# Attention scores by head on 64 rows of the matmul array each, 128 queries at a time, with one maximum for both heads

## The chip, the cores and the metric

The kernel runs on one core of one Trainium2 chip. The metric is the device time of one execution in microseconds. Before the change the median of three runs is 1036.53 us (1034.72 to 1038.2).

## The reference, cut to what matters

Batch 4, 8 heads, 576 positions, head width 64. Each head's attention output is mixed with a memory readout, and the result goes through two dense feed-forward layers (512 to 2048 to 512, over 2304 tokens).

```python
scores = scale * np.matmul(q, k.transpose(0, 1, 3, 2))        # scale = 1/8
scores = np.where(causal, -1000000000.0, scores)              # causal: key after query
a = np.exp(scores - scores.max(-1, keepdims=True))
a /= a.sum(-1, keepdims=True) + 1e-09
local = np.matmul(a, v)
mem_out = (phi(q) @ M_prev) / (phi(q) . z_prev + 1e-6)        # phi(x) = elu(x) + 1
x = g * mem_out + (1 - g) * local                             # g = sigmoid(beta), by head
h = x @ w_in;  x = (h * sigmoid(h)) @ w_out                   # first layer
h = x @ w2_in; y = (h * tanh(softplus(h))) @ w2_out           # second layer
```

## The kernel before

**Stages.** The heads are worked in 16 pairs: the two heads of a pair lie one above the other on the 128 partitions (64 of head width each). A *visit* is a pair with some of its query tiles, a *step* is one tile of 128 queries of a visit (qt = 0 to 4; the last has 64 queries). Batch 0 is visited twice, first for qt 0 and 1 of its four pairs (steps 0 to 7), then for qt 2 to 4 (steps 8 to 19); batches 1 to 3 follow pair by pair with all five (steps 20 to 79). A step goes through `stage_a` (scores, maximum, exponentials, a split of the result into two float16 parts, and a DMA that transposes them), `stage_b` (times v, the memory product, normalization) and, every second step, `stage_c` (transpose by TensorE, then a DMA to `xd` in DRAM).

The first layer reads `xd` in nine *chunks* of 256 tokens, each with 8 steps of `gemm1`, `hidden` and `gemm2`. Chunk 1 needs qt 2 and 3 of all four pairs of batch 0, chunk 2 needs qt 4 of these and qt 0 and 1 of all four pairs of batch 1. The weights of both layers are loaded, scaled and split by ScalarE and VectorE ahead of use; those of the first layer are prepared beside the first twenty steps. The second layer starts when the first is done.

**Scores before (L495 to L551).** A step works on two tiles of 64 queries. For each, the stationary operand has 128 columns in which the queries of the two heads alternate (`"p q e -> p (q e)"`), with zeros where a column's head is not that of the partition, so that one product over all 128 rows gives both heads' scores, 64 queries by 2 heads on the 128 output partitions. A tile i has 64(i+1) keys. For qt 0 and 1 the product is in float32 (TensorE runs it as two passes); for qt 2 to 4 both operands are split into two fp32r parts and three products are added. A last product of `ident16` with a 64-column `mask` adds the causal mask. Then, by tile, VectorE takes the maximum (L538, with a read of its accumulator behind it), ScalarE the exponentials (L543), ScalarE or VectorE the first float16 part (L545) and VectorE the rest (L546).

The operands with their zeros are prepared by `prep_q` (L448): a copy for each head, and for qt 2 to 4 the rest by GpSimd or VectorE (`rest`, L356).

**PSUM.** Scores of steps 0 to 7 take turns over four banks (2 to 5, `s_all`), those of later steps over two (4 and 5, `s_few`, L789). The two tiles of qt 0 or 1 share one bank; each tile of qt 2 and 3 takes one; qt 4 (576 keys) takes two.

**Order.** All instructions are handed to `Plan`, which puts them in order by a simulation of the engines with given costs: the operation with the lowest priority value that is ready goes next. On TensorE attention goes ahead of `gemm1` and `gemm2` (priority 1e6 and more); on ScalarE and VectorE the work of the first layer (`MOE_B`, -1e6) and of the weights goes ahead of attention from step 8 on. Each engine then runs its list in order. `mm` (L360) gives the planner the cost of products.

Of the kernel before, what the change touches and what calls it, by code (L numbers as in the profile page):

```python
# [173 lines left out]
def attn_moe_moe2_kernel(ctx: ExitStack, tc: tile.TileContext, kq, vm, beta, w1, w2, out):  # L174
# [22 lines left out]
    def buf(name, shape, dt, n=1):  # L197
        ts = [sb.tile([128, *shape], dt, name=f"{name}_{i}") for i in range(n)]
        return ts

    def ring(tiles):
        state = [0]

        def take():
            state[0] += 1
            return tiles[(state[0] - 1) % len(tiles)]

        return take
# [5 lines left out]

    ident, = buf("ident", [128], F32)
    ident16, = buf("ident16", [128], BF16)
    mask, = buf("mask", [D], BF16)
    gb, = buf("gb", [H], F32)
    gv, = buf("gv", [H // 2, 4], F32)
    eps, = buf("eps", [4], F32)  # L220
# [46 lines left out]
    pt_tile, = carve([PT_BLOCKS, 128], F16)  # L267
    kqr, rmr, rvr = ring(carve([2, S], F32, 2)), ring(carve([130], F32, 3)), ring(carve([VM - 130], F32, 2))
    khr, klr = ring(carve([S], F32R, 2)), ring(carve([S], F32R, 2))
    q_parts = [(0, 4), (4, 5)]  # L270
    qz = [[carve([4, D, 2], F32) for _ in range(2)], [carve([5, D, 2], F32R, 2)]]
    qr = [ring(t) for t in qz]
    v1s, v2s = carve([NQ, 2, D + 2], F16, 2), carve([NQ, 2, D], F16, 2)
    v1r, v2r = ring(v1s), ring(v2s)
    scales = carve([4], F32, 3)
    scr, topr, scaler, gvr = ring(scales), ring(carve([2], BF16, 3)), ring(carve([1], F32, 3)), ring(carve([4], F32, 3))
    er_ = ring(carve([S], F32, 2))
    jr = ring(carve([576], BF16))
    pr, phr = ring(carve([640], F32, 4)), ring(carve([16, 128], F16, 3))
    mr = ring(carve([1], F32, 4))  # L280
    t4r = ring(carve([2, 4, D], F32))
    denr, xr = ring(carve([2, 4], F32, 2)), ring(carve([2, 2, D], F32))
    xor_ = ring(carve([256], F32, 2))
# [14 lines left out]
    def cols(a):  # L298
        n = 1
        for x in a.shape[1:]:  # L300
            n *= x
        return n
# [53 lines left out]
    def rest(prio, out, in_, hi, es=("POOL", "DVE")):  # L356

        tt(prio, out, in_, hi, ALU.subtract, es)

    def mm(prio, ms, whole=False):  # L360

        ns, edge, before = 0, None, 0
        for o, _, r, _, _ in ms:
            n = cols(o)
            load, one, times = (107, 2 * n / 2.4 + 2.5, 2) if r.dtype == F32 else (107 if r.dtype == F32R else 14, n / 2.4 + 2.5, 1)
            for _ in range(times):
                ns += one + (0 if edge is None else max(0, load - before))
                edge = (edge or (load, 0))[0], one
                before = one

        def go():
            for o, l, r, a, z in ms:
                nc.tensor.matmul(out=o, lhsT=l, rhs=r, start=a, stop=z)  # L373

        writes = [m[0] for m in ms]
        if whole:
            writes = [(t, 0, 128, b0 // 2048 * 2048, -(-b1 // 2048) * 2048) for t, _, _, b0, b1 in map(plan.region, writes)]
        plan.add(prio, [("PE", ns, go)], writes, [x for m in ms for x in m[1:3]], edge=edge)
# [13 lines left out]
    def setup():  # L392
        p = -1e9
        other(p, "SP", 100, lambda: nc.scalar.dma_start(out=gb, in_=beta), [gb])
        for x, t in enumerate([t for j in qz for i in j for t in i]):
            for r, e in ((slice(0, 64), 1), (slice(64, 128), 0)):
                o = t[r, :, :, e].bitcast(F32)
                plan.add(p + x, [
                    ("DVE", 0.52 * cols(o) + 68, lambda o=o: nc.vector.memset(o, 0.0)),
                    ("POOL", 1.0 * cols(o) + 60, lambda o=o: nc.gpsimd.memset(o, 0.0))], [t[r]], [])  # L400

        def consts():
            make_identity(nc, ident16)
            nc.gpsimd.memset(mask, 0.0)

            nc.gpsimd.affine_select(
                out=mask, in_=mask, compare_op=ALU.is_ge, fill=-8e9, base=0,
                pattern=[[-2, D]], channel_multiplier=1)
            make_identity(nc, ident)
            nc.gpsimd.memset(eps[:, 0:2], 1e-9 * PSCALE)  # L410
            nc.gpsimd.memset(eps[:, 2:4], 1e-6)
            nc.gpsimd.memset(ones, 1.0)
            nc.gpsimd.memset(onesf, 1.0)
            for t in scales:
                nc.gpsimd.memset(t[:, 2:4], 1.0)
            for t in v1s:
                nc.gpsimd.memset(t[:, :, :, D:D + 1], 1.0)

        other(p, "POOL", 2000, consts, [ident16, mask, ident, eps, ones, onesf, *scales, *v1s])
        act(p, gb, gb, AF.Tanh, 0.5)  # L420
        g3 = gb.rearrange("p (a h) -> p a h", h=2)
        ts(p, gv[:, :, 0:2], g3, -0.5, ALU.mult, 0.5, ALU.add)
        ts(p, gv[:, :, 2:4], g3, 0.5, ALU.mult, 0.5, ALU.add)
# [22 lines left out]
        dma(prio, rm[v], vm[p, :, 0:130], reads=[])  # L446

    def prep_q(v, j, prio):  # L448
        i0, n = q_parts[j]
        parts = qq[v, j] = qr[j]()  # L450
        for e in range(2):
            r = slice(64 * e, 64 * e + 64)
            src = rq[v][r, 64 * i0:64 * (i0 + n)].rearrange("p (i q) -> p i q", q=64)
            hi = parts[0][r, :, :, e]
            copy(prio, hi, src)
            if j:
                rest(prio, parts[1][r, :, :, e], src, hi, QL)

    def prep_k(v, prio):
        n = min(S, 128 * VISITS[v][2])  # L460
# [34 lines left out]
    def stage_a(n, sbk, prio):  # L495

        v, qt = STEPS[n]
        kh, kl = kk.get(v, (None, None))
        tiles = [i for i in (2 * qt, 2 * qt + 1) if i < S // 64]
        nk = qt + 1  # L500
        nb = 2 * len(tiles) * nk
        ph = phr()[:, 0:nb, :]
        pv = ph.rearrange("p (s k t) c -> p s k t c", s=2, k=nk)

        ns = [64 * (i + 1) for i in tiles]
        one_bank = sum(ns) <= 512
        scs, masks, ms = [], [], []
        for t, (i, N) in enumerate(zip(tiles, ns)):
            if N > 512 and turn[0] % 2:
                turn[0] += 1  # L510
            off = 0
            if t and one_bank:
                off = ns[0]
            else:
                bk = sbk[turn[0] % len(sbk)]
                turn[0] += 1 if N <= 512 else 2
            sc = bk[0][:, bk[1] + off:bk[1] + off + N]
            scs.append(sc)
            j = 0 if i < 4 else 1
            qs = [x[:, i - q_parts[j][0]].rearrange("p q e -> p (q e)") for x in qq[v, j]]  # L520
            new = not (t and one_bank)
            m = []
            for a, z in [(0, min(N, 512))] + ([(512, N)] if N > 512 else []):
                if j == 0:
                    m.append((sc[:, a:z], qs[0], rk[v][:, a:z], new, False))
                else:
                    m += [(sc[:, a:z], qs[0], kh[:, a:z], new, False), (sc[:, a:z], qs[0], kl[:, a:z], False, False),
                          (sc[:, a:z], qs[1], kh[:, a:z], False, z < N)]
            ms.append(m)
            masks.append((sc[:, N - 64:N], ident16, mask, False, not one_bank or t == len(tiles) - 1))  # L530
        if one_bank:
            mm(prio, sum(ms, []) + masks)
        else:
            for m, x in zip(ms, masks):
                mm(prio, m + [x])
        for t, (N, sc) in enumerate(zip(ns, scs)):
            m1, junk, P = mr(), jr()[:, 0:N], pr()
            other(prio, "DVE", 1.04 * N + 225, lambda m1=m1, sc=sc, junk=junk: nc.vector.tensor_scalar(  # L538
                out=junk, in0=sc, scalar1=-0.125, scalar2=None, op0=ALU.mult, op1=ALU.min, accum_out=m1), [m1, junk], [sc])
            if N < 128 * nk:  # L540
                pad = P[:, N:128 * nk]
                other(prio, "POOL", 90, lambda pad=pad: nc.gpsimd.memset(pad, 0.0), [pad])
            act(prio, P[:, 0:N], sc, AF.Exp, 0.125, m1)  # L543
            Pv = P[:, 0:128 * nk].rearrange("p (k c) -> p k c", c=128)
            copy(prio + D_S, pv[:, 0, :, t, :], Pv, PSCALE)  # L545
            stt(prio + D_S, pv[:, 1, :, t, :], Pv, PSCALE, pv[:, 0, :, t, :], ALU.mult, ALU.subtract)  # L546

        live = pt_live[1 - LAG:]
        p0 = next(x for x in [pt_live[-1][1], 0] + [z for _, z in live] if x + nb <= PT_BLOCKS and all(
            z <= x or x + nb <= a for a, z in live))  # L550
        pt_live.append((p0, p0 + nb))  # L551
        pt = pts[n] = pt_tile[:, p0:p0 + nb, :]
        plan.add(prio, [("SP", max(1180, 400 + 113 * nb), lambda: nc.sync.dma_start_transpose(
            out=pt, in_=ph.rearrange("p n c -> p (n c)")))], [pt], [ph], tail=112 * nb)
# [5 lines left out]
    def stage_b(n, prio):  # L560
# [3 lines left out]
        nk = qt + 1  # L564
        v1, v2, gvv = vv[v]
        vb = bank[6 + qt % 2]
        pw = pts.pop(n).rearrange("p (s k t) (q e) -> p s k e (t q)", s=2, k=nk, e=2)
        ms = []
        for e in range(2):
            o = vb[0:R, 65 * e:65 * e + 65]  # L570
# [215 lines left out]
    load_kq(0, -1e8)  # L786
    setup()

    s_all, s_few = [[(banks, 512 * i) for i in r] for r in (range(2, 6), range(4, 6))]  # L789
    prep(0, -1e6)  # L790
    load_vm(0, -1e6)

# [111 lines left out]
```

## Time and profile before

| | |
|---|---|
| median of three runs | 1036.53 us |
| profiled execution | 1037.78 us |
| its span, first to last instruction | 1036.0 us |
| granted TensorE clock, mean | 0.965 |
| TensorE busy | 952.9 us (92%) |
| VectorE, ScalarE, GpSimd busy | 645.3, 659.1, 295.9 us |

The span is what the trace covers; the run's time is 1.8 us more. Busy times are unions of an engine's instructions. A product's recorded duration contains its way through the array, so what a product costs a busy TensorE is read from the start of one to the start of the next.

### The profile page before, as it was taken

The page shows a single profiled execution, that of the slowest core. Times are in us where ns is not written, and L with a number is a line of the kernel's source. Part 1 is how long each engine was busy: PE and PEld are TensorE (multiplying, and loading weights), DVE is VectorE, ACT ScalarE, POOL GpSimd, SP SyncE. Part 2 cuts the span into 40 slices and gives each one's busy share as a digit, 9 for nine tenths or more (in the row PEclk, how much of TensorE's full clock was granted, in tenths as well). Part 3 has the DMA queues.
Part 4 walks back from the last instruction along what each step waited for, and adds up shares of the span by engine and source line. Part 5 has one row for each costly group of instructions (what it writes and reads, how often), then busy time and mean ns, then how long its engine had stood idle before and what let it go on. Part 6 is the DMA issues. An engine that isn't in the chain of part 4 may idle for free.

```text
span 1036.0 us, 20987 instructions
## 1 busy us (share of the span) xinstructions
PE 952.9 (92%) x8352; PEld 752.8 (73%) x8352; DVE 645.3 (62%) x1379; ACT 659.1 (64%) x1134; POOL 295.9 (29%) x361
## 2 busy tenths in 40 slices
PE   3344979799999999999999999999999999999998
PEld 2233868688888888888888888766676766666664
DVE  7897876777878767667676641644545445544433
ACT  8977876677777767767766752645645445555544
POOL 1132333244434334332222221212212122222221
PEclk9955889899999999999999999999999999999999
DMA  9749648866757866554424200200100001000000
GB/s 306 239 128 226 190 126 161 173 144 138 165 122 133 155 144 120 101 137 150 166 80 158 88 22 1 62 21 22 41 7 35 22 22 41 22 21 21 2 21 21
DMA packets 143153, 102.39 MB, mean 99 GB/s; under 512 B 110544, under 2 KB 132560, under 8 KB 138960
## 3 DMA queue, kind: packets, MB, share of 16 engines
q1 hardware_dynamic: 142912, 101.06, 38.5%
q8 instruction: 65, 1.06, 0.4%
q14 instruction: 32, 0.26, 0.1%
q10 hardware_dynamic: 144, 0.00, 0.0%
HBM read 60.67 MB, written 14.16 MB: 72 GB/s over the span
## 4 chain that ended last, share of the span: by engine, by line
PE 75%; issue 2%; DMA 2%; ACT 1%; DVE 1%; POOL 1%; POOLq 0%; SPq 0%; ACTq 0%; DVEq 0%
PE banks L373 74%; PE banks L601 1%; POOL g L326 1%; DMA ws<-w 1%; DMA arena<-arena 1%; DMA yd<-w 0%; ACT arena L312 0%; DVE arena L320 0%; ACT xh L312 0%; ACT ga L312 0%; DVE ga L320 0%; ACT w L312 0%; DVE xh L320 0%; POOLq L900 0%; DVE arena L538 0%
## 5 line engine op out<-in xcount | busy, mean ns | idle before, releaser
L373 PEld LDWEIGHTS <-w 128*128 128x128 f16 x3456 | 333.8, 99 | 49.8 <-issue 6.5
L373 PEld LDWEIGHTS <-arena 128*128 128x128 f16 (+1 forms) x3168 | 224.4, 101 | 84.1 <-DMA arena<-arena 31.4
L326 POOL TENSOR_TENSOR g<-ga,g 128x512 f16<-128x512 f32 x108 | 138.4, 1282 | 351.4 <-ACT g L312 346.3
L373 PE MATMUL banks<-xh,w 128*128 128x256 f16 x1728 | 212.2, 275 | 3.7 <-ACT xh L312 2.0
L373 PE MATMUL banks<-g,w 128*128 128x256 f16 x1728 | 210.3, 274 | 5.0 <-ACT w L312 3.5
L373 PE MATMUL banks<-xh,arena 128*128 128x256 f16 x1728 | 199.1, 273 | 0.0
L373 PE MATMUL banks<-arena,g 128*128 128x512 f16 x864 | 198.2, 379 | 0.6 <-POOL g L326 0.6
L373 PE MATMUL banks<-arena 128*128 128x65 f16 (+9 forms) x1728 | 117.4, 224 | 46.6 <-DMA arena<-arena 29.8
L373 PEld LDWEIGHTS <-g 128*128 128x128 f16 x864 | 84.4, 98 | 88.0 <-POOL g L326 1.1
L320 DVE SCALAR_TENSOR_TENSOR ga<-ga,banks 128x512 f32<-128x512 f32 x108 | 73.9, 685 | 98.3 <-ACT ga L312 97.7
L312 ACT ACTIVATE arena<-arena 128x256 f16<-128x256 f32 (+8 forms) x230 | 116.9, 524 | 25.3 <-DMA arena<-kq 9.7
L312 ACT ACTIVATE ga<-ga 128x512 f32<-128x512 f32 x108 | 67.4, 628 | 76.2 <-DVE ga L317 54.1
L320 DVE SCALAR_TENSOR_TENSOR arena<-arena 128x512 f16<-128x512 f32 (+6 forms) x184 | 111.5, 616 | 5.7 <-ACT arena L312 5.4
L312 ACT ACTIVATE w<-w 128x512 f32<-128x512 f32 x108 | 66.8, 626 | 51.7 <-DVE w L317 27.0
L312 ACT ACTIVATE arena<-banks,arena 128x64 f32<-128x64 f32 (+8 forms) x144 | 74.0, 522 | 25.8 <-DVE arena L538 22.2
L373 PE MATMUL banks<-arena_r 128*128 128x512 f32 (+4 forms) x288 | 78.5, 393 | 10.3 <-ACT arena L312 6.6
L312 ACT ACTIVATE g<-ga 128x512 f16<-128x512 f32 x108 | 67.5, 626 | 30.0 <-DVE ga L320 28.0
L312 ACT ACTIVATE ga<-banks,xsc 128x512 f32<-128x512 f32 x72 | 49.3, 685 | 57.9 <-PE banks L373 56.1
L538 DVE TENSOR_SCALAR_CACHE_REDUCE arena<-banks 128x64 bf16<-128x64 f32 (+8 forms) x144 | 69.3, 481 | 24.7 <-PE banks L373 17.6
L326 POOL TENSOR_TENSOR g<-w,g 128x512 f16<-128x512 f32 x36 | 41.6, 1156 | 134.3 <-ACT g L312 134.3
L326 POOL TENSOR_TENSOR arena_r<-arena,arena_r 64x320 fp32r<-64x320 f32 (+1 forms) x48 | 56.6, 1178 | 39.4 <-ACT arena_r L312 33.3
L326 POOL TENSOR_TENSOR arena<-arena 128x256 f32<-128x256 f32 (+1 forms) x48 | 39.6, 825 | 94.7 <-DVE arena L326 80.8
(97 smaller groups left out, 939.6 us busy)
## 6 DMA issues: line engine op xcount, KB each, us to landing
ws<-w SPq DMA_DIRECT2D x28, 1024.0 KB, 5.0
arena<-kq SPq DMA_DIRECT2D x16, 576.0 KB, 4.2
arena<-vm SPq DMA_DIRECT2D x16, 325.0 KB, 3.3
xs<-xd SPq DMA_DIRECT2D x9, 512.0 KB, 4.2
yd<-w SPq DMA_DIRECT2D x36, 128.0 KB, 1.8
xs<-yd SPq DMA_DIRECT2D x9, 512.0 KB, 3.8
y<-w SPq DMA_DIRECT2D x18, 256.0 KB, 2.0
xd<-arena SPq DMA_DIRECT2D x32, 128.0 KB, 1.9
```

The lines of the kernel that those rows point to most:

```text
L312: return ("ACT", ns, lambda: nc.scalar.activation(out=out, in_=in_, func=func, scale=scale, bias=bias))
L320: return ("DVE", 1.04 * cols(out) + 160, lambda: nc.vector.scalar_tensor_tensor(out=out, in0=in0, scalar=s, in1=in1, op0=op0, op1=op1))
L326: return (e, ns, lambda: eng.tensor_tensor(out=out, in0=in0, in1=in1, op=op))
L373: nc.tensor.matmul(out=o, lhsT=l, rhs=r, start=a, stop=z)
L538: other(prio, "DVE", 1.04 * N + 225, lambda m1=m1, sc=sc, junk=junk: nc.vector.tensor_scalar(out=junk, in0=sc, scalar1=-0.125, scalar2=Non ...
L601: plan.add(prio, [("PE", 56, lambda o=o, x2=x2: nc.tensor.transpose(o, x2, ident[0:R, 0:R]))], [o], [x2, ident], edge=(107, 56))
```

## The change

For qt 0 to 3 a step works on 128 queries of each head in separate products: head e has its queries and keys on partitions 64e to 64e+63, uses these 64 rows of the array only, and writes 128 queries to its own PSUM bank, with 128(qt+1) keys. The heads' products are issued in turn. The operands need no zeros; the scale 1/8 goes into the queries. The mask is one 128-column product for each head. One VectorE instruction takes the maxima of both heads; ScalarE takes the exponentials of each head; the copy and the rest are one instruction each for both heads. qt 4 keeps the alternate form, head by head instead of query by query. Every step takes a pair of banks: (2,3) and (4,5) in turn for steps 0 to 7, (4,5) alone afterwards. The ring of exponentials holds 2 tiles of 1024 instead of 4 of 640. The planner counts a product over 64 rows at half its cost.

```diff
-    mask, = buf("mask", [D], BF16)
+    mask, = buf("mask", [128 + D], BF16)
...
-    pr, phr = ring(carve([640], F32, 4)), ring(carve([16, 128], F16, 3))
-    mr = ring(carve([1], F32, 4))
+    pr, phr = ring(carve([1024], F32, 2)), ring(carve([16, 128], F16, 3))
+    mr = ring(carve([2], F32, 3))
...
-                ns += one + (0 if edge is None else max(0, load - before))
+                ns += (one + (0 if edge is None else max(0, load - before))) * l.shape[0] / 128
...
     def prep_q(v, j, prio):
...
+        if j == 0:
+            qq[v, 0] = q1r()
+            copy(prio, qq[v, 0], rq[v][:, 0:256], 0.125)
+            return
+        src, q2 = rq[v][:, 256:512], q2r()
+        qq[v, 1] = q2[:, 0], q2[:, 1]
+        copy(prio, q2[:, 0], src, 0.125)
+        stt(prio, q2[:, 1], src, 0.125, q2[:, 0], ALU.mult, ALU.subtract)
         for e in range(2):
             r = slice(64 * e, 64 * e + 64)
...
+            src, hi, lo = rq[v][r, 512:576], q4s[0][r, e], q4s[1][r, e]
+            copy(prio, hi, src, 0.125)
+            stt(prio, lo, src, 0.125, hi, ALU.mult, ALU.subtract)
...
     def stage_a(n, sbk, prio):
...
+        if qt < 4:
+
+            scs = [banks[:, b0 + 512 * e:b0 + 512 * e + N] for e in range(2)]
+            ms, nb = [], 4 * nk
+            for e, sc in enumerate(scs):
+                r, c = slice(64 * e, 64 * e + 64), slice(128 * (qt % 2), 128 * (qt % 2) + 128)
+                if qt < 2:
+                    ms.append([(sc, qq[v, 0][r, c], rk[v][r, 0:N], True, False)])
                 else:
+                    kh, kl, (qh, ql) = *kk[v], qq[v, 1]
+                    ms.append([(sc, qh[r, c], kh[r, 0:N], True, False), (sc, qh[r, c], kl[r, 0:N], False, False),
+                               (sc, ql[r, c], kh[r, 0:N], False, False)])
+            masks = [(sc[:, N - 128:N], ident16, mask[:, 0:128], False, True) for sc in scs]
+            mm(prio, [x for y in zip(*ms) for x in y] + masks)
...
+        other(prio, "DVE", 1.04 * cols(both) + 146, lambda: nc.vector.tensor_reduce(
+            out=m1, in_=both, axis=AX, op=ALU.max, negate=True), [m1], [both])
+        for o, sc, m in tiles:
+            act(prio, o, sc, AF.Exp, 1.0, m)
+        copy(prio + D_S, ph_[:, 0], P, PSCALE)
+        stt(prio + D_S, ph_[:, 1], P, PSCALE, ph_[:, 0], ALU.mult, ALU.subtract)
...
-    s_all, s_few = [[(banks, 512 * i) for i in r] for r in (range(2, 6), range(4, 6))]
+    s_all, s_few = [2, 4], [4]
```

## Rows read from the trace of the kernel before

**Rows 1.** Windows by stage: busy us of each engine, granted clock, DMA share.

```profile
0.00:104.00 104.00, 40.45 (x241) 31.39 (x242) 87.04 (x200) 84.06 (x142) 23.55 (x54) 0.77 0.78 225
...
204.00:445.00 241.00, 240.03 (x2712) 208.82 (x2709) 179.37 (x530) 173.05 (x359) 96.03 (x144) 1.00 0.66 133
```

**Rows 2.** Groups by form on TensorE, 204 to 445 us.

```profile
L373 PE MATMUL banks<-arena_r 128*128 128x384 f32 x30 | 7.7, 364 | 0.0
```

**Rows 3.** Timeline of TensorE, 400 to 425 us: start, duration, merged products.

```profile
403.83 0.61 PE L373 MATMUL banks<-arena 128*128 128x64 f32 x4
...
404.34 0.49 PE L373 MATMUL banks<-xh,w 128*128 128x256 f16 x3
404.67 0.92 PE L373 MATMUL banks<-arena 128*128 128x192 f32 x4
...
405.48 1.01 PE L373 MATMUL banks<-arena 128*128 128x65 f16 x20
...
407.12 0.68 PE L373 MATMUL banks<-arena_r 128*128 128x320 f32 x3
...
407.68 0.49 PE L373 MATMUL banks<-xh,w 128*128 128x256 f16 x3
...
411.58 0.77 PE L373 MATMUL banks<-arena_r 128*128 128x384 f32 x3
...
412.23 1.15 PE L373 MATMUL banks<-xh,w 128*128 128x256 f16 x9
...
416.47 0.93 PE L373 MATMUL banks<-arena_r 128*128 128x512 f32 x3
...
417.28 0.82 PE L373 MATMUL banks<-xh,w 128*128 128x256 f16 x6
```

**Rows 4.** Timeline of TensorE around a 128-row and a 64-row transpose.

```profile
406.33 0.27 PE L601 MATMUL banks<-ident,arena 128*128 128x128 f32 x1
406.44 0.49 PE L373 MATMUL banks<-xh,w 128*128 128x256 f16 x3
...
420.50 0.27 PE L601 MATMUL banks<-ident,arena 64*128 64x64 f32 x1
420.70 0.50 PE L373 MATMUL banks<-g,w 128*128 128x256 f16 x3
```

**Rows 5.** Timeline of weight loads (PEld) around the same two transposes.

```profile
406.00 0.30 PEld L373 LDWEIGHTS banks<-arena 128*128 128x128 f32 x2
...
406.22 0.14 PEld L601 LDWEIGHTS banks<-ident,arena 128*128 128x128 f32 x1
...
420.07 0.30 PEld L373 LDWEIGHTS banks<-arena 128*128 128x128 f32 x2
420.49 0.13 PEld L601 LDWEIGHTS banks<-ident,arena 64*128 64x128 f32 x1
```

**Rows 6.** Groups by form on VectorE, ScalarE and GpSimd, 204 to 445 us.

```profile
L538 DVE TENSOR_SCALAR_CACHE_REDUCE arena<-banks 128x512 bf16<-128x512 f32 x11 | 7.5, 683 | 2.0 <-PE banks L373 1.8
L538 DVE DVE_READ_ACCUMULATOR arena<-banks 128x1 f32 x92 | 7.5, 81 | 0.0
L538 DVE TENSOR_SCALAR_CACHE_REDUCE arena<-banks 128x256 bf16<-128x256 f32 x10 | 4.2, 420 | 3.8 <-ACT arena L312 3.7
...
L312 ACT ACTIVATE arena<-arena 128x512 f16<-128x512 f32 x21 | 13.1, 625 | 0.3
L312 ACT ACTIVATE arena<-arena 128x256 f16<-128x256 f32 x20 | 8.3, 413 | 0.3
...
L326 POOL TENSOR_TENSOR arena_r<-arena,arena_r 64x320 fp32r<-64x320 f32 x20 | 18.0, 901 | 12.8 <-ACT arena_r L312 12.2
```

**Rows 7.** Timeline from the mask of a qt 4 step to its exponentials.

```profile
400.84 0.21 PE L373 MATMUL banks<-mask,ident 128*128 128x64 bf16 x1
...
402.56 0.72 ACT L312 ACTIVATE arena<-banks,arena 128x576 f32<-128x576 f32 x1
```

**Rows 8.** Instructions on the first layer's input: `gemm1` products (first count) of chunk 1.

```profile
203.60:275.40 71.80, 22.98 (x179) 1.22 (x1) 1.14 (x1) 1.00 0.68 138
```

**Rows 9.** Timeline of VectorE: the last preparation of chunk 2.

```profile
274.18 1.27 DVE L320 SCALAR_TENSOR_TENSOR xh<-xs,xsc,xh 128x1024 f16<-128x1024 f32 x1
```

More of the change, by code (lines that the diff above doesn't have):

```diff
@@ L269, in attn_moe_moe2_kernel @@
     khr, klr = ring(carve([S], F32R, 2)), ring(carve([S], F32R, 2))
-    q_parts = [(0, 4), (4, 5)]
-    qz = [[carve([4, D, 2], F32) for _ in range(2)], [carve([5, D, 2], F32R, 2)]]
-    qr = [ring(t) for t in qz]
+    q1r, q2r, q4s = ring(carve([256], F32, 2)), ring(carve([2, 256], F32R, 2)), carve([2, D], F32R, 2)
     v1s, v2s = carve([NQ, 2, D + 2], F16, 2), carve([NQ, 2, D], F16, 2)
@@ L277, in attn_moe_moe2_kernel @@
     er_ = ring(carve([S], F32, 2))
-    jr = ring(carve([576], BF16))
-    pr, phr = ring(carve([640], F32, 4)), ring(carve([16, 128], F16, 3))
-    mr = ring(carve([1], F32, 4))
+    pr, phr = ring(carve([1024], F32, 2)), ring(carve([16, 128], F16, 3))
+    mr = ring(carve([2], F32, 3))
     t4r = ring(carve([2, 4, D], F32))
@@ L362, in mm @@
         ns, edge, before = 0, None, 0
-        for o, _, r, _, _ in ms:
+        for o, l, r, _, _ in ms:
             n = cols(o)
@@ L394, in setup @@
         other(p, "SP", 100, lambda: nc.scalar.dma_start(out=gb, in_=beta), [gb])
-        for x, t in enumerate([t for j in qz for i in j for t in i]):
+        for x, t in enumerate(q4s):
             for r, e in ((slice(0, 64), 1), (slice(64, 128), 0)):
-                o = t[r, :, :, e].bitcast(F32)
+                o = t[r, e].bitcast(F32)
                 plan.add(p + x, [
@@ L404, in consts @@
             nc.gpsimd.memset(mask, 0.0)
-            nc.gpsimd.affine_select(
-                out=mask, in_=mask, compare_op=ALU.is_ge, fill=-8e9, base=0,
-                pattern=[[-2, D]], channel_multiplier=1)
+            for r, c, n in ((slice(0, 128), 0, 128), (slice(0, 64), 128, D), (slice(64, 128), 128, D)):
+                m = mask[r, c:c + n]
+                nc.gpsimd.affine_select(
+                    out=m, in_=m, compare_op=ALU.is_ge, fill=-1e9, base=0, pattern=[[-1, n]], channel_multiplier=1)
             make_identity(nc, ident)
@@ L448, in prep_q @@
     def prep_q(v, j, prio):
-        i0, n = q_parts[j]
-        parts = qq[v, j] = qr[j]()
+        if j == 0:
[6 more added lines that the diff above has]
+        stt(prio, q2[:, 1], src, 0.125, q2[:, 0], ALU.mult, ALU.subtract)
         for e in range(2):
             r = slice(64 * e, 64 * e + 64)
[L453 to L457, printed above, removed]
+            src, hi, lo = rq[v][r, 512:576], q4s[0][r, e], q4s[1][r, e]
+            copy(prio, hi, src, 0.125)
+            stt(prio, lo, src, 0.125, hi, ALU.mult, ALU.subtract)
     def prep_k(v, prio):
@@ L497, in stage_a @@
         v, qt = STEPS[n]
-        kh, kl = kk.get(v, (None, None))
-        tiles = [i for i in (2 * qt, 2 * qt + 1) if i < S // 64]
         nk = qt + 1
[L501 to L525, printed above, removed]
-                else:
[L527 to L530, printed above, removed]
@@ L531, in stage_a @@
-        if one_bank:
-            mm(prio, sum(ms, []) + masks)
-        else:
[L534 to L546, printed above, removed]
+        N = min(S, 128 * nk)
@@ new lines, in stage_a @@
+        b0 = 512 * sbk[turn[0] % len(sbk)]
+        turn[0] += 1
+        ph, P, m1 = phr(), pr(), mr()
+        if qt < 4:
[5 more added lines that the diff above has]
+                    ms.append([(sc, qq[v, 0][r, c], rk[v][r, 0:N], True, False)])
+                else:
+                    kh, kl, (qh, ql) = *kk[v], qq[v, 1]
[3 more added lines that the diff above has]
+            mm(prio, [x for y in zip(*ms) for x in y] + masks)
+            both = banks[:, b0:b0 + 1024].rearrange("p (e c) -> p e c", e=2)[:, :, 0:N]
+            P = P[:, 0:2 * N].rearrange("p (e c) -> p e c", e=2)
+            ph_ = ph[:, 0:nb].rearrange("p (s e k) c -> p s e (k c)", s=2, e=2)
+            tiles = [(P[:, e], scs[e], m1[:, e:e + 1]) for e in range(2)]
+        else:
+            nb = 2 * nk
+            both = banks[:, b0:b0 + N]
+            kh, kl = kk[v]
+            hi, lo = [t.rearrange("p e q -> p (e q)") for t in q4s]
+            ms = []
+            for a, z in ((0, 512), (512, N)):
+                ms += [(both[:, a:z], hi, kh[:, a:z], True, False), (both[:, a:z], hi, kl[:, a:z], False, False),
+                       (both[:, a:z], lo, kh[:, a:z], False, z < N)]
+            mm(prio, ms + [(both[:, N - 64:N], ident16, mask[:, 128:192], False, True)])
+            pad = P[:, N:128 * nk]
+            other(prio, "POOL", 90, lambda: nc.gpsimd.memset(pad, 0.0), [pad])
+            tiles = [(P[:, 0:N], both, m1[:, 0:1])]
+            P = P[:, 0:128 * nk]
+            ph_ = ph[:, 0:nb].rearrange("p (s k) c -> p s (k c)", s=2)
@@ L548, in stage_a @@
+        m1 = m1[:, 0:len(tiles)]
+        other(prio, "DVE", 1.04 * cols(both) + 146, lambda: nc.vector.tensor_reduce(
[4 more added lines that the diff above has]
+        stt(prio + D_S, ph_[:, 1], P, PSCALE, ph_[:, 0], ALU.mult, ALU.subtract)
+        ph = ph[:, 0:nb]
         live = pt_live[1 - LAG:]
@@ L566, in stage_b @@
         vb = bank[6 + qt % 2]
-        pw = pts.pop(n).rearrange("p (s k t) (q e) -> p s k e (t q)", s=2, k=nk, e=2)
+        if qt < 4:
+            pw = pts.pop(n).rearrange("p (s e k) q -> p s k e q", s=2, e=2)
+        else:
+            pw = pts.pop(n).rearrange("p (s k) (e q) -> p s k e q", s=2, e=2)
         ms = []
```

## The prediction

> **What bounds the kernel now.** I read the page's slices first, then the busy times by stage, then TensorE's own start-to-start times around the scores. The stages differ. From 204 to 445 us, while attention and the first layer run side by side, TensorE is busy 240.0 of 241 us at full clock, with VectorE at 179 and ScalarE at 173 [rows 1]: the end moves there only by what TensorE has to do, or by a gap that is put into it. Behind 445 us the page's slices show TensorE just as full, with work that the change doesn't touch. In the first 104 us it is the other way round: TensorE 40 us, VectorE 87, ScalarE 84, granted clock 0.77 [rows 1]. There the end moves by ScalarE, VectorE and the latency of a step. The forecast has one term for each of these stages.
>
> Ten pairs have their scores in the saturated stage: three 384-column products a pair, 30 recorded [rows 2]. The other six come before it.
>
> **Scores on TensorE, before.** From the first product of a group to the first product behind its mask [rows 3]: qt 0 404.34 - 403.83 = 0.51 us, qt 1 0.81, the tiles of 320, 384 and 512 keys 0.56, 0.65 and 0.81, and that of 448 between its neighbours at 0.73. So qt 0 to 3 cost 0.51 + 0.81 + 1.21 + 1.54 = 4.07 us a pair. Without a mask at about 0.03, an fp32r product is 0.21 us at 384 columns and 0.26 at 512. A float32 pass is (0.81 - 0.05) / (2 x 448) = 0.85 ns a column.
>
> **Scores on TensorE, after.** A step has the same products for each head, over 128(qt+1) columns: two float32 passes a head in qt 0 and 1, three fp32r products a head in qt 2 and 3. What this costs hangs on one thing that no row shows: whether the two heads' products, on different rows of the array, run side by side.
> - One behind the other: qt 0 4 x 128 x 0.85 = 0.44, qt 1 0.87, qt 2 6 x 0.21 = 1.26, qt 3 6 x 0.26 = 1.56. Sum 4.13.
> - Side by side: 0.22, 0.44, 0.63, 0.78. Sum 2.07. In float32 the turns don't mesh, since a head's two passes follow each other in the list: of four passes, the second of one head and the first of the other share a slot, and three slots are left. That makes qt 0 0.33 and qt 1 0.65, sum 2.39.
>
> I take 2.23, between the last two: the heads share neither operand partitions nor a bank, and TensorE already overlaps what doesn't collide, with 208.8 us of loads beside 240.0 us of products [rows 1]. The first bound stays for the range, with about one chance in five. By the Trainium skill (TensorEngine Tiling (Array Packing), Key Properties) different tiles of the array load weights and multiply in parallel; by that the sum would be 2.07 to 2.39, and no run here shows it yet.
>
> **What is added on TensorE.** Going from 128 rows to 64 and back. The trace has it at the 64-row transposes: from two loads of the same kind to the transpose 0.43 us instead of 0.33 [rows 4, 5], and from the transpose to the next product 0.20 instead of 0.11 [rows 4]. The load of the 64-row transpose starts with it (420.49 and 420.50), that of the 128-row one 0.11 ahead [rows 4, 5]. So a visit costs 0.19 us more at least; if in a step the whole 0.20 of both sides is lost, 0.40. I take 0.20, the row itself. Before there were none in the scores; now there are four a pair. The eight masks grow from 64 columns to 128: a 256-column product takes (1.15 - 0.27) / 8 = 0.11 us [rows 3], so one is 0.055 and a step's two 0.11.
>
> Sum after: 2.23 + 4 x (0.20 + 0.11) = 3.47 us a pair, 0.60 less than 4.07. Ten pairs: **-6.0 us**. With 0.40 a switch it is +2; with perfect meshing and 0.19, -7.6; with the heads one behind the other and 0.20, 4.13 + 1.24 - 4.07 = +1.3 a pair, **+13** (and +21 with 0.40). qt 4 keeps its products, and `stage_b` its product count; the transposing DMAs keep their size.
>
> **The other engines.** Nine maxima a pair become five. From 256 to 512 columns one grows by 0.263 us, so 0.157 is fixed [rows 6]; the change saves 4 x 0.157 and nine reads of the accumulator at 0.081, and pays 256 more columns (0.26): -1.1 us. Four copies and four rests fewer, at a fixed 0.20 each from 413 and 625 ns [rows 6]: -0.8 on ScalarE and about as much on VectorE. Exponentials: 256 more columns, +0.2. `prep_q`: GpSimd loses two rests of 0.90 [rows 6]; VectorE takes over one of 256 columns (0.42) and two of 64 (0.2 each), +0.8; ScalarE swaps two copies of 256 and two of 320 for two of 256 and two of 64, -0.5. So a pair saves about 1.1 us on each of ScalarE and VectorE and 1.8 on GpSimd.
>
> Behind 204 us this is hidden by TensorE. Ahead of it four to five pairs' worth, up to 5 us on each, can come through. The first layer starts when chunk 0 is prepared, chunk 1 when batch 0 is through, and both engines idle 15 to 20% up to 104 us [rows 1], so that part of it only lengthens waits. I take **-2 us** (0 to -5).
>
> **The banks.** From step 8 on a step takes both banks until its second exponential is read, where before the tiles took turns. A qt 4 step, which held both already, needs 402.56 + 0.72 - 400.84 = 2.44 us from mask to the end of its exponentials [rows 7], of which 0.72 + 0.75 (a 576-column maximum by the slope above) + about 0.35 of hand-over are its own, leaving 0.6 of queueing. With 0.6 to 1.2 of queueing, the steps of a pair hold the banks for products (3.5 + 1.1), maxima (five at 0.157 and 3136 columns at 1.03 ns: 4.0), exponentials (nine at 0.24 fixed and 3136 columns at 0.83 ns: 4.8), hand-over and waiting for TensorE (5 x 0.7) and queueing (3 to 6): 19 to 22 us. The attention before goes at 241 / 10 = 24 us a pair [rows 1, 2]. It fits, barely. Who waits: the scores of the next step stand in TensorE's list, and behind them `gemm1` and `gemm2`. If the list is right they fill the time, except where the first layer runs out: at chunk 2. Its input is ready at 275.45 [rows 9], when 179 recorded of chunk 1's 192 `gemm1` products are done [rows 8], so 13 x 0.11, twice with `gemm2`: under 3 us of cover. A pace of 2 us a pair slower over the 2.5 pairs between would cost 5 - 3 = 2 us and the time that TensorE saved there. I take **+2** (0 to +6).
>
> **Sum.** -6 - 2 + 2 = -6 us on the profiled execution's 1037.8, which lies 1.3 above the median of the runs: 1031.8 by the profile, 1030.5 by the median. I forecast **1031**.
>
> **The rivals.**
> 1. *The heads' products run one behind the other.* For it: no row shows two at once, and products on all rows start in order. Against: separate partitions and banks. It decides by one thing, the second head's start: a whole product behind the first (0.16 us or more at 384 columns). Then +13 of TensorE time, -2 at the start, no gap at chunk 2: 1031 + 19 - 2 = 1048. Chance 0.19.
> 2. *The bank pair sets the pace.* If queueing is nearer 2 us a step, a pair takes 27 us instead of 24, chunk 2 comes 2.5 x 3 = 7 us late against 3 of cover, and the 1.5 us saved over these pairs is a gap too; the start of chunk 1 suffers likewise in steps 8 to 19. +8 in all against the sum: 1039. For it: two banks held for the whole of a 1024-column maximum and two exponentials. Against: a tile before held its bank for 2.4 us and more, and fewer instructions shorten the queues. Chance 0.17.
> 3. *The start gains more.* If the wait for chunks 0 and 1 is all ScalarE and VectorE, the full 5 us come through, and of GpSimd's 4.5 x 1.8 = 8 us, for whose rests TensorE waits, half: 1031 - 3 - 4 = 1024. For it: the two engines' share of the first 104 us [rows 1]. Against: their idle fifth. Chance 0.14.
> 4. *Loads stand in the way.* If a head's next load had to wait for its own product, each product would cost a load of 0.11 more: over the 12 slots of a pair 2.23 + 1.32 = 3.55, the sum 4.79 a pair, +7 for -6 and no gap at chunk 2: 1031 + 13 - 2 = 1042. Against it are the 208.8 us of loads beside products over all rows [rows 1] and the load 0.11 us ahead of the 128-row transpose [rows 4, 5]. Chance 0.07. The Trainium skill states it so (TensorE: Matmul & The Clock Gate, The mechanism): a load overlaps products in flight only when it is for other rows; the rows here disagree.
>
> **How the numbers follow.** Forecast 0.43, rivals 0.19, 0.17, 0.14 and 0.07. About 3 us (0.3%) is what a measurement tells from no change, that is 1033.4 to 1039.6. The forecast's own range is 1026 to 1035, with 0.33 of its 0.43 below 1033.4; with rival 3, faster is 0.47. Slower are rivals 1 and 4 and half of rival 2, which lies on the bound: 0.34. The rest is 0.19. The range reaches from just below rival 3 to rival 1: 1021 to 1048.
>
> **What would show it.** Right: the heads' products start within some 0.02 us of each other, the groups of qt 2 and 3 take about 0.95 and 1.1 us to the product behind their masks, TensorE stays without gaps from 200 us on, and chunk 2 is prepared before 275. Wrong: start-to-start of a full product between the heads; a wait of TensorE for ScalarE's exponentials ahead of scores; a gap at chunk 2; switches of over 0.3 us.

## The result, and the profile after

The changed kernel takes 1046.58 us (median of four runs, 1045.56 to 1048.26), the one before 1037.37 us in the same comparison: a ratio of 1.0095, 95% interval 1.007 to 1.012. It is slower by 9.2 us where 6 us less were forecast. The profiled execution took 1047.29 us, its span is 1045.5 us, 9.5 more than before.

Two of the three terms came with the forecast's sign. The page's slices of the kernel after show where the third went: each digit is a slice of 26 us, and the eleventh (261 to 287 us) stands at 6 on TensorE and, with the next, at 8 in its granted clock; before both rows had a 9 there.

```profile
PE   2436888899699999999999999999999999999998
...
PEclk9956979799889999999999999999999999999999
```

The windows of the kernel after, cut there (busy us of TensorE, weight loads, VectorE, ScalarE, GpSimd, each with its count of instructions; then the granted clock, the DMA share and GB/s), beside [rows 1]:

```profile
0.00:104.00 104.00, 45.70 (x288) 30.89 (x289) 89.11 (x162) 83.32 (x135) 15.48 (x37) 0.77 0.80 234
204.00:276.00 72.00, 69.11 (x779) 56.58 (x777) 52.13 (x106) 45.93 (x92) 24.58 (x27) 1.00 0.57 127
276.00:296.00 20.00, 13.90 (x91) 9.97 (x92) 12.28 (x29) 9.00 (x16) 3.13 (x5) 0.57 0.73 150
296.00:445.00 149.00, 148.97 (x1660) 124.42 (x1657) 105.49 (x219) 98.80 (x188) 46.29 (x52) 1.00 0.58 119
```

From 276 to 296 us TensorE is busy 13.9 of 20 us, and 10.9 of that at a granted clock of 1.2 GHz: the clock is 0.50 from 278 to 295 us, 0.57 over the whole 20.

```profile
278.00:295.00 17.00, 10.90 (x68) 8.01 (x67) 11.13 (x25) 7.10 (x12) 2.24 (x3) 0.50 0.70 146
```

It falls where a gap of over 4 us begins; from 204 to 276 us TensorE had been idle 2.9 of 72 us. Before, it was full at 2.4 GHz through all of this stage. The timeline of TensorE there, with the idle time before a group and what ended it:

```profile
275.87 1.43 PE L370 MATMUL banks<-arena_r 64*128 64x512 f32 x6 [0.88 <-ACT arena L309]
277.24 0.29 PE L370 MATMUL banks<-mask,ident 128*128 128x128 bf16 x2
277.36 0.65 PE L370 MATMUL banks<-arena 128*128 128x65 f16 x8
282.26 0.80 PE L370 MATMUL banks<-diag,onesf 128*128 128x128 f32 x2 [4.26 <-DVE diag L323]
...
289.47 0.80 PE L370 MATMUL banks<-xh,w 128*128 128x256 f16 x3 [0.83 <-DVE xh L317]
```

TensorE has no product of the first layer left and waits for chunk 2 (`diag` and `xh` are written on the way from `xd` to a chunk that `gemm1` can read). What answers to [rows 8, 9], in the windows of the layer's input and VectorE's timeline: from chunk 1's input to chunk 2's all of chunk 1's products are done, where 13 were left before, and the last piece of chunk 2 ends at 289.41 instead of 275.45.

```profile
199.10:289.40 90.30, 24.91 (x193) 1.27 (x1) 1.13 (x1) 0.94 0.60 130
```

```profile
197.78 1.28 DVE L317 SCALAR_TENSOR_TENSOR xh<-xs,xsc,xh 128x1024 f16<-128x1024 f32 x1
...
288.13 1.28 DVE L317 SCALAR_TENSOR_TENSOR xh<-xs,xsc,xh 128x1024 f16<-128x1024 f32 x1
```

With these two marks the whole difference can be laid out. Before, chunk 1 was ready at 203.58, by this row of the kernel before:

```profile
202.30 1.28 DVE L320 SCALAR_TENSOR_TENSOR xh<-xs,xsc,xh 128x1024 f16<-128x1024 f32 x1
```

Chunk 2 was ready 71.9 us later, and the rest took 760.5; after, 199.06, 90.3 and 756.1. So: the start 4.5 us shorter, the stretch between the two chunks **18.5 us longer**, what follows 4.4 us shorter. Sum +9.6, the span's +9.5 but for rounding. Of the stretch between the chunks TensorE was idle 0.04 us before and 8.9 us after.

The scores themselves, on TensorE, for a step of qt 2 and one of qt 3 [rows 3]:

```profile
404.70 0.38 PE L370 MATMUL banks<-g,w 128*128 128x256 f16 x2
405.01 0.79 PE L370 MATMUL banks<-arena_r 64*128 64x384 f32 x6
405.74 0.29 PE L370 MATMUL banks<-mask,ident 128*128 128x128 bf16 x2
405.86 2.13 PE L370 MATMUL banks<-g,w 128*128 128x256 f16 x18
...
409.55 0.97 PE L370 MATMUL banks<-arena_r 64*128 64x512 f32 x6
410.46 0.29 PE L370 MATMUL banks<-mask,ident 128*128 128x128 bf16 x2
```

Six products of 384 columns, three for each head, take 0.73 us to the mask; before, three took 0.61 (from 411.58 [rows 3] to the mask at 412.19): the heads run side by side. A window of the first 0.01 us of the 384-column row holds two products, so both heads have started in it:

```profile
405.01 0.44 PE L370 MATMUL banks<-arena_r 64*128 64x384 f32 x2
```

Attention's pace is read from the exponentials of qt 4, one a pair. ScalarE's timeline for pairs 6 and 16, the kernel before and then the kernel after: 23.5 us a pair before (24 was read from [rows 1, 2]), 25.7 after.

```profile
210.88 0.73 ACT L312 ACTIVATE arena<-banks,arena 128x576 f32<-128x576 f32 x1
...
445.48 0.74 ACT L312 ACTIVATE arena<-banks,arena 128x576 f32<-128x576 f32 x1
```

```profile
213.24 0.74 ACT L309 ACTIVATE arena<-banks,arena 128x576 f32<-128x576 f32 x1 [0.48 <-DVE arena L541]
...
470.05 0.74 ACT L309 ACTIVATE arena<-banks,arena 128x576 f32<-128x576 f32 x1
```

### The profile page after: what moved, and what is told of

It reads as the page before. It is cut to its first block, busy times and chain, and to the rows that moved or that the text cites. A ratio compares the mean times of both kernels' runs of the same rounds, so it can differ in the third digit from the quotient of the medians.

```text
span 1045.5 us, 20536 instructions
## 1 busy us (share of the span) xinstructions
PE 955.8 (91%) x8352; PEld 736.4 (70%) x8352; DVE 661.9 (63%) x1156; ACT 641.4 (61%) x1064; POOL 262.9 (25%) x268
## 4 chain that ended last, share of the span: by engine, by line
PE 78%; DMA 7%; ACT 6%; DVE 3%; issue 3%; POOL 1%; SPq 0%; POOLq 0%; DVEq 0%; ACTq 0%
PE banks L370 77%; DMA ws<-w 3%; ACT arena L309 2%; ACT w L309 1%; DMA arena<-arena 1%; PE banks L605 1%; ACT ws L667 1%; DMA xd<-arena 1%; DMA g<-w 1%; DMA xs<-xd 1%; DVE arena L317 1%; POOL g L323 1%; DVE w L317 1%; DVE arena L541 0%; DMA arena<-kq 0%
## 5 line engine op out<-in xcount | busy, mean ns | idle before, releaser
L370 PE MATMUL banks<-xh,w 128*128 128x256 f16 x1728 | 209.5, 274 | 2.8 <-DVE xh L317 1.9
L370 PE MATMUL banks<-xh,arena 128*128 128x256 f16 x1728 | 199.1, 273 | 0.0
L370 PE MATMUL banks<-arena 128*128 128x65 f16 (+7 forms) x1728 | 115.3, 232 | 49.9 <-ACT arena L309 29.9
L309 ACT ACTIVATE arena<-arena 128x640 f16<-128x640 f32 (+7 forms) x146 | 94.7, 667 | 28.9 <-PE banks L370 16.1
L317 DVE SCALAR_TENSOR_TENSOR arena<-arena 128x640 f16<-128x640 f32 (+7 forms) x120 | 98.9, 831 | 14.7 <-ACT arena L309 14.4
L309 ACT ACTIVATE arena<-banks,arena 128x128 f32<-128x128 f32 (+4 forms) x144 | 73.6, 546 | 42.8 <-DVE arena L541 39.7
L541 DVE TENSOR_REDUCE arena<-banks 128x2 f32<-128x256 f32 (+4 forms) x80 | 64.3, 803 | 25.6 <-PE banks L370 22.5
L323 POOL TENSOR_TENSOR arena<-arena 128x256 f32<-128x256 f32 (+1 forms) x48 | 42.2, 879 | 119.4 <-DVE arena L323 61.5
L370 PE MATMUL banks<-arena_r 64*128 64x384 f32 (+3 forms) x288 | 56.9, 419 | 12.0 <-ACT arena L309 11.0
L314 DVE TENSOR_SCALAR ga<-banks,xsc 128x512 f32<-128x512 f32 x36 | 27.0, 750 | 50.3 <-PE banks L370 50.0
```

The lines of the kernel that those rows point to most:

```text
L309: return ("ACT", ns, lambda: nc.scalar.activation(out=out, in_=in_, func=func, scale=scale, bias=bias))
L314: return ("DVE", ns, lambda: nc.vector.tensor_scalar(out=out, in0=in0, scalar1=s1, scalar2=s2, op0=op0, **kw))
L317: return ("DVE", 1.04 * cols(out) + 160, lambda: nc.vector.scalar_tensor_tensor(out=out, in0=in0, scalar=s, in1=in1, op0=op0, op1=op1))
L323: return (e, ns, lambda: eng.tensor_tensor(out=out, in0=in0, in1=in1, op=op))
L541: other(prio, "DVE", 1.04 * cols(both) + 146, lambda: nc.vector.tensor_reduce(out=m1, in_=both, axis=AX, op=ALU.max, negate=True), [m1], [ ...
```

## The experiments

Three theories stood against each other. *Bank theory*: from step 8 on one pair of banks serves all steps, so that the next scores wait for the last exponential; attention gets slower and chunk 2 late. *Vector theory*: the 1024-column maxima and the rests moved to VectorE slow it. *List theory*: with 64-row products at half price the planner's order is wrong for the chip. "The kernel before" took 1038.2 to 1038.4 us in these comparisons, and the ratios are to it.

**1. The held pair alone.** The kernel before, with all its products, maxima and copies; the banks go by pair and step, and for that the products of a step's two tiles become one entry of TensorE's list, as they are in the changed kernel.

```diff
-        writes = [m[0] for m in ms]
+        writes = [m[0] for m in ms] if hold is None else [hold]
...
-            if N > 512 and turn[0] % 2:
-                turn[0] += 1
...
+                if t == 0 and turn[0] % 2:
+                    turn[0] += 1
                 bk = sbk[turn[0] % len(sbk)]
+                if t == 0:
+                    pair = banks[:, bk[1]:bk[1] + 1024]
-                turn[0] += 1 if N <= 512 else 2
+                turn[0] += 2 if one_bank or N > 512 else 1
...
+        mm(prio, sum(ms, []) + masks if one_bank else [y for m, x in zip(ms, masks) for y in m + [x]], hold=pair)
```

> The kernel before, with the products, maxima and copies of before, but each step takes both banks of a pair until its last exponential is read. Bank theory (the pair sets attention's pace and makes chunk 2 late): chunk 2 prepared 8 us or more later than 275.5, a gap on TensorE at chunk 2, 1042 to 1052 us. Vector theory (the long maxima and the rests moved to VectorE are what slows attention) and list theory (the half price in the planner spoils the order): none of theirs is in it, so 1037 +-3 us and chunk 2 at 275 +-3.

1059.04 us, ratio 1.0197 (1.0166 to 1.0228): 21 us slower than before, more than the whole change. Its last piece of chunk 2 and its window there:

```profile
297.62 1.28 DVE L320 SCALAR_TENSOR_TENSOR xh<-xs,xsc,xh 128x1024 f16<-128x1024 f32 x1
```

```profile
276.00:299.00 23.00, 16.40 (x161) 12.91 (x161) 15.74 (x50) 14.87 (x32) 6.03 (x12) 0.85 0.75 153
```

Chunk 1 is ready at 205.6, chunk 2 93.3 us later (71.9 before), and TensorE is idle 6.6 of the 23 us ahead of it. Attention runs at 26.2 us a pair (224.27 to 486.27 for the same ten). That is the changed kernel's picture without any of its arithmetic. The bank theory's size was too small (1042 to 1052); the others had no change here (1037 +-3). Some 2.5 of the 21 us are a wait near the end that runs without a held pair have too (see 8).

**2. The full price in the planner.**

```diff
-                ns += (one + (0 if edge is None else max(0, load - before))) * l.shape[0] / 128
+                ns += (one + (0 if edge is None else max(0, load - before)))
```

> The changed kernel with the planner's full price for products over 64 rows. List theory: the order gets right, the gap at chunk 2 goes, 1030 to 1038 us. Bank theory and vector theory: the pace stays, chunk 2 prepared within 4 us of 289, 1044 to 1050 us.

1042.09 us, ratio 1.0040 (1.002 to 1.006): 4.5 us better than the change. Chunk 2 is ready at 283.6, the pace is 24.4 us a pair. Neither expectation was met (1030 to 1038 by the list theory, 1044 to 1050 by the others): the time lies between the two. So another order of the list can take away a part of the loss; whether it does so by being the right price, 8 and 10 tell.

**3 and 4. Batch 1 in two visits**, which needs only qt 0 and 1 of its pairs ahead of chunk 2: in the changed kernel, and as the control in the one before.

```diff
-SPLIT = 1
+SPLIT = 2
```

> The changed kernel with batch 1 also visited twice (qt 0 and 1 of its four pairs first), so that chunk 2 needs two steps of each pair instead of five. If the loss is that chunk 2 comes late (bank and vector theory alike): no gap between 270 and 290 us, TensorE's saving stays, 1026 to 1034 us. If the loss is spread over the stage (list theory, or more work on TensorE than read): 1042 us or more.

> The control for that: the kernel before with batch 1 visited twice. It has no gap at chunk 2, so nothing is won there: 1036 to 1042 us by all theories (two to five us for eight more loads and preparations). Under 1033 us, the split helps by itself, and the run of the changed kernel with it has to be set against this one.

The changed kernel with it takes 1032.91 us, ratio 0.9948 (0.993 to 0.9967): 13.7 us less than without, and faster than the kernel before. The kernel before with it takes 1045.24, ratio 1.0077 (1.0051 to 1.0103): 7 us more. So the split doesn't help by itself; it helps where chunk 2 is late. In the changed kernel the chunk is ready at 247.9 now, and the stretch that had the gap is full at full clock:

```profile
246.65 1.27 DVE L317 SCALAR_TENSOR_TENSOR xh<-xs,xsc,xh 128x1024 f16<-128x1024 f32 x1
```

```profile
276.00:296.00 20.00, 20.00 (x225) 16.31 (x225) 12.29 (x29) 12.13 (x27) 7.08 (x8) 1.00 0.72 157
```

With both visits split, the change is worth 12.3 us by the medians and 11.1 by the profiled spans: 5.2 up to chunk 1 (197.9 against 203.0) and 5.9 behind it. The control's own loss is part of that, and it is more than expected (1036 to 1042). Its trace shows where: TensorE is idle 81.1 us ahead of chunk 1, 76.1 in the kernel before, and 2.5 us more near the end (see 8). Why it is, no run here says. Against the kernel before, the change with the split is worth 5.3 us.

**5. Two steps in one pair of banks.** qt 0 takes the first half of each bank, qt 1 the second, from step 8 on.

```diff
+        h0 = 256 * (qt % 2) if qt < 2 and n >= N0 else 0
...
-            scs = [banks[:, b0 + 512 * e:b0 + 512 * e + N] for e in range(2)]
+            scs = [banks[:, b0 + h0 + 512 * e:b0 + h0 + 512 * e + N] for e in range(2)]
...
```

> The changed kernel; from step 8 on qt 0 uses the first half of each bank of the pair and qt 1 the second, so that these two steps don't wait for each other. Two of a pair's five handovers of the banks go. Bank theory: the pace falls from 25.7 us a pair by 1 to 2, chunk 2 prepared 3 to 6 us earlier than 289, 1040 to 1044 us. List theory alone, or vector theory: 1045 to 1048 us.

1040.11 us, ratio 1.0015 (0.9996 to 1.0034), 24.3 us a pair (206.38 to 449.74), chunk 2 at 284.9: as the bank theory had it, with nothing changed on VectorE or in prices. Chunk 1 came later here than in the changed kernel (203.4 for 199.1), so that the stretch between the chunks fell from 90.3 to 81.5 us. The vector theory is needed neither for the loss in 1 nor for the gain here.

**6. Maximum and exponentials ahead of the first layer's work.**

```diff
-        other(prio, "DVE", 1.04 * cols(both) + 146, lambda: nc.vector.tensor_reduce(
+        ahead = prio - (3e6 if n >= N0 else 0)
+        other(ahead, "DVE", 1.04 * cols(both) + 146, lambda: nc.vector.tensor_reduce(
...
-            act(prio, o, sc, AF.Exp, 1.0, m)
+            act(ahead, o, sc, AF.Exp, 1.0, m)
```

> The changed kernel; from step 8 on maximum and exponentials go ahead of the first layer's work on VectorE and ScalarE, so that the banks come free sooner. Bank theory: a shorter hold (about 1 us a step less), pace below 24 us a pair, chunk 2 near 280, 1036 to 1042 us. Vector theory: VectorE's amount of work is the same, so 1044 us or more. Against both: hidden comes later, and the first layer waits for it.

1055.77 us, ratio 1.0168 (1.0141 to 1.0195). A miss for the bank theory's number; the vector theory had 1044 or more. The pace did get better, 24.9 us a pair, but chunk 1 came at 211.3 and chunk 2 at 303.6: what now goes first stands ahead of the chunks' own preparation and of the later stages of attention too. The run mixes both and doesn't decide between the theories by itself.

**7. The heads one behind the other in the list.**

```diff
-            mm(prio, [x for y in zip(*ms) for x in y] + masks)
+            mm(prio, [x for y in ms for x in y] + masks)
```

> The changed kernel with all products of head 0 ahead of those of head 1. If it takes the turns to have two heads at once: groups of qt 2 and 3 (six products) grow from 0.94 and 1.11 us to about 1.5 and 1.9, those of qt 0 and 1 (two passes each, issued as one product) stay at 0.64 and 0.85; 1.4 us a pair more on TensorE, 1052 to 1062 us. If products overlap in any order: no change, 1045 to 1048 us.

1047.35 us, ratio 1.0086 (1.0064 to 1.0109): no change from the changed kernel. Its trace has the six products of qt 2 in the same time, 0.73 us to the mask:

```profile
300.25 0.80 PE L370 MATMUL banks<-arena_r 64*128 64x384 f32 x6
300.98 0.28 PE L370 MATMUL banks<-mask,ident 128*128 128x128 bf16 x2
```

The second product of the trace starts 10 ns behind the first, with three products of one head in the list ahead of the other's. It must be the other head's first, since the starts come in pairs, and from pair to pair 0.16 us and more go by; the trace itself doesn't name the head. The turns aren't needed.

**8. Split and full price.** Both edits in the changed kernel.

> The changed kernel with batch 1 visited twice and the full price in the planner, the two that helped, together. If the half price costs by making attention late for chunk 2, the split has taken that away already: 1031 to 1034 us, as with the split alone. If it costs by a worse order all along: 1027 to 1030 us.

1035.89 us, ratio 0.9981 (0.9964 to 0.9997): 3 us more than with the split alone, where the same or less had been expected. One wait makes up most of it. Near the end of this run TensorE waits for ScalarE, in the second layer, whose work the two edits leave as it is:

```profile
1024.78 0.60 PE L370 MATMUL banks<-arena,g 128*128 128x512 f16 x2 [2.50 <-ACT g L309]
```

The profiles of 1, 4, 5, 6 and 10 have the same wait of 2.5 us; those of the kernel before, of the changed kernel and of the other runs have not. That it comes with some orders of the list and not with others is the likely reading; each profile is of one execution.

**9 and 10. Split and shared pair**, and the full price with them.

> The changed kernel with batch 1 visited twice and with qt 0 and 1 sharing the pair of banks: the two that shorten attention's way to chunk 2 by the bank theory. If the split has already taken away all that late attention costs: 1030 to 1034 us, as with the split alone. If the start (chunks 0 and 1) is paced by the banks too: chunk 1 ahead of 196 us, 1025 to 1030 us.

> The same with the full price in the planner. If the price has no steady effect (with it 4 us less alone, 3 us more beside the split): within 4 us of the run without, either way.

1034.50 us, ratio 0.9970 (0.9955 to 0.9984), and 1037.89, ratio 0.9994 (0.9982 to 1.0006). Sharing brings nothing any more once chunk 2 is early, and chunk 1 is ready at 202.6, not ahead of 196 as it would be if the banks paced the start. The full price is 3 us worse here, as in 8, and 4.5 better in 2: it has no steady sign. What it does is another order of the same work, and such orders differ by some 4 us, 2.5 of them by the wait shown in 8, which 10 has and 9 has not.

**11. The held pair with the split**, in the kernel before.

> The kernel before with the pair held by each step (21 us slower than before) and batch 1 visited twice. If what the held pair costs is the late chunk 2: no gap there, and about what the split kernel before took, 1041 to 1048 us. If a slower pace costs by itself, in a stage where TensorE has other work: 1055 us or more.

1042.76 us, ratio 1.0042 (1.0028 to 1.0056): of the held pair's 21 us, 16 are gone, and it is no slower than the split kernel before without the pair (1045.24). Attention is as slow as in 1, about 25.8 us a pair over batches 2 and 3, but TensorE is full where the gap was:

```profile
276.00:296.00 20.00, 20.00 (x244) 17.41 (x243) 16.84 (x42) 13.53 (x32) 9.17 (x13) 1.00 0.60 136
```

So a slower pace shows no loss as long as TensorE has other work. At least 16 of its 21 us came through one place, chunk 2.

**12. Three tiles for the exponentials.**

```diff
-    pr, phr = ring(carve([1024], F32, 2)), ring(carve([16, 128], F16, 3))
+    pr, phr = ring(carve([1024], F32, 3)), ring(carve([16, 128], F16, 3))
```

> The changed kernel with three tiles of 1024 for the exponentials instead of two. If the exponentials wait for a free tile rather than the scores for banks: shorter holds, pace below 25 us, 1035 to 1043 us. Bank theory: the tile is free when the banks are, 1043 to 1049 us.

1049.52 us, ratio 1.0111 (1.0093 to 1.0128), chunk 2 at 291.4: no better than with two tiles, so it isn't the ring of tiles.

## Why the prediction was wrong

**The step that failed is the one on the banks: "It fits, barely ... I take +2 (0 to +6)".** The stretch between chunks 1 and 2 grew by 18.5 us. In the terms of the sum, the span's +9.5 is -4.5 at the start, -2.4 for products (below) and so about +16 for the banks, where +2 was put down. The mechanism was there as rival 2, with chunk 2 named as the place; its price (+8) and its chance (0.17) were too low. Three things were missed:
- *The pace.* The banks were put at 19 to 22 us a pair against a pace of 24; the terms as listed add up to 20 to 23, and the pace before was 23.5. After, it is 25.7. The time that the banks are held was right: over pairs 6 to 15 of the kernel after, from a step's first product to the end of its last exponential, the timelines of TensorE and ScalarE give 20.4 us a pair. What was left out is the time from there to the next step's first product, 5.3 us a pair or 1.1 a step; the 0.7 a step for hand-over and waiting for TensorE stood for waits within the hold. The next scores are one entry of TensorE's list and stand behind whatever the list has ahead of them. For instance the exponentials of pair 8's qt 2 end at 254.66, TensorE starts six products of the first layer at 254.70, and the scores of qt 3 start at 255.45:

```profile
253.61 1.05 ACT L309 ACTIVATE arena<-banks,arena 128x384 f32<-128x384 f32 x2
```

```profile
254.70 0.82 PE L370 MATMUL banks<-xh,w 128*128 128x256 f16 x6
255.45 0.96 PE L370 MATMUL banks<-arena_r 64*128 64x512 f32 x6
```

- *The way from the scores to the chunk.* The fourth pair of batch 1 had its qt 1 scores 8.6 us later than before (at 245.40 for 236.79), the chunk came 14 us later. The layer's input waits in SyncE's queue, too. In the kernel before it is issued at 262.58, 2.0 us after the `xd` write that it needs; in the kernel after at 273.96, behind two `yd` writes, a load and a transpose, 4.4 us after its own. First before, then after:

```profile
260.61 0.32 SPq L383 DMA_DIRECT2D xd<-arena  x1
262.15 0.33 SPq L383 DMA_DIRECT2D arena<-kq  x1
262.58 0.40 SPq L383 DMA_DIRECT2D xs<-xd  x1
```

```profile
269.52 0.72 SPq L380 DMA_DIRECT2D xd<-arena  x1
270.33 0.89 SPq L380 DMA_DIRECT2D yd<-w  x2
271.38 1.21 SPq L380 DMA_DIRECT2D arena<-kq  x1
272.68 1.19 SPq L554 DMA_TRANSPOSE arena<-arena  x1
273.96 0.53 SPq L380 DMA_DIRECT2D xs<-xd  x1
```

- *What a gap costs.* TensorE is idle 2.9 us from 204 to 276 and 6.1 from 276 to 296, and 10.9 us of its work run at 1.2 GHz. What that costs can be read from the scores of qt 4, six products to the mask: 1.92 us there (286.23 to 288.15), 1.02 at 2.4 GHz (259.66 to 260.68). So the 10.9 us would have been some 5 less, an estimate, and idle time and clock together make up 14 of the 16 us. The forecast priced a gap at its length.

**TensorE's saving had the right mechanism and the wrong size.** The heads run side by side, as forecast with four chances in five. From the last product ahead of a group to the first behind its masks, less the 0.109 us of one 256-column product, medians over the groups between two such products behind 204 us (of qt 3 there is one): after 0.64, 0.85, 0.94 and 1.11 for qt 0 to 3, 3.54 a pair; forecast 3.47. But the same measure gives 3.78 for before, not 4.07: there a group's first fp32r product starts 0.03 us behind the product ahead of it, which has its 0.109 still to run. In the trace of the kernel before:

```profile
399.78 0.27 PE L373 MATMUL banks<-g,w 128*128 128x256 f16 x1
399.81 1.19 PE L373 MATMUL banks<-arena_r 128*128 128x512 f32 x6
```

So 0.08 us too much were counted for each of four tiles, and a pair saves 0.24 us instead of 0.60, ten pairs 2.4 instead of 6.0. That 3.54 comes so near 3.47 is luck, since two errors cancel. The switch was put at 0.20 and costs 0.30: the product ahead of a 64-row group takes 0.20 us instead of 0.11, the first pair of 384-column products 0.28 where the next takes 0.17 (before, the first one took 0.26 but started 0.08 early), and behind the group the mask comes 0.27 after the start of the last pair. The products were put too high: 0.21 for one of 384 columns, which takes 0.17 to 0.18 from start to start, after as before, and three slots for float32, which needs two. (The sum's best case, -7.6, should read -8.0 by its own terms.)

**The start** was forecast at -2 and gave -4.5 (chunk 1 at 199.06 for 203.58). That ScalarE's and VectorE's smaller load does it wasn't tried by itself. Nor is it shown that the gain belongs to the change: in 3 and 4 it is there, 5.2 us at chunk 1, but the other runs put chunk 1 at 195.7 to 211.3 with the change (10 and 6) and at 198.1 to 205.7 without it (11 and 1). An order of the list alone moves it as far.

**The rivals.** The first (heads one behind the other) is ruled out by the pair of starts, the fourth (loads in the way) by the same groups: with a load of 0.11 us for each turn qt 2 would take 1.3 us where it took 0.94. The third (the start gains more) came nearer at chunk 1 than the forecast did, and it missed the time all the same. The Trainium skill warns of what happened, in general words (TensorEngine Tiling (Array Packing), Gotcha 1: PSUM Pressure): row tiling puts different row tiles into different banks and so raises the pressure on PSUM. The runs agree as to the banks: holding a pair of them a step, with the products of before, cost 21 us in run 1. The prediction drew on that page for the products alone.

Open stays what brings the wait of 2.5 us near the end of some runs, what moves chunk 1, and why splitting batch 1 leaves TensorE idle 5 us more ahead of it in the kernel before.

## What to carry to other kernels

Here two products on different rows of the array took two banks at once; before that is bought, count who else wants the banks, and what waits at the end of the stage that gets slower. Count the hold and also the time until the next step takes the banks over. A stage may lose pace without a loss that shows while the bound engine has other work, and lose 16 us and more where that work runs out: look for that place, and take the wait away there (here by doing first what the next chunk needs), and the same change turns from 9 us slower to 5 us faster. And before a few us are put down to an edit, look for a wait elsewhere that came with another order of the list.

## What the runs showed of the hardware

- Products of 64 rows on different halves of the array ran at once whatever their order in the list: starts 4 ns apart in turn, 10 ns apart with three products of one head ahead of the other's (run 7). The two passes of a float32 product meshed as well: qt 0's four passes of 128 columns started in two pairs, 7 ns apart within a pair and 0.21 us from pair to pair, where three slots had been forecast.
- Going from 128 rows to 64 and back cost a group of such products 0.30 us, not only the 0.19 that a single 64-row transpose shows [rows 4, 5]: 0.09 on the product ahead, 0.11 on the first pair, 0.10 ahead of the mask.
- Weight loads for the same 64 rows ran ahead of the product in flight: six loads of a qt 2 step within 0.47 us from the first product's start.
